# Lightning attention and a snake MLP: partition halves that hold two neighbouring blocks instead of two head groups

## The chip, the core and the metric

The kernel runs on one core of a Trainium2 chip. The metric is the device time of one execution in microseconds (us). Five engines run side by side, each through its own list of instructions in order: TensorE (PE, matmuls; PEld is its weight load), VectorE (DVE), ScalarE (ACT), GpSimd (POOL) and SyncE (SP), which here does nothing but issue transfers. The transfers themselves run on 16 DMA engines. An engine whose next instruction waits for a semaphore stands still, and everything behind that instruction in its list stands still with it.

## The reference

Four batches, eight heads, 768 positions, head width 64. Each head keeps a state of 64x64; blocks of positions are worked off in order, and the output feeds an MLP.

```
for each block of 64 positions:
    intra = ((q k^T) * lam**(i-j), lower triangle) v
    inter = (q * lam**(i+1)) state
    out   = intra + inter
    state = lam**64 * state + (k * lam**(63-j))^T v
x = out as 3072 tokens x 512 (8 heads x 64)
h = x @ w_in                       # 512 -> 2048
g = h + sin(alpha*h)**2 / (alpha + 1e-9)
result = g @ w_out                 # 2048 -> 512, float32
```

## The kernel before, in words

**Attention.** The kernel uses blocks of 128 positions: 6 to a batch (NB), 24 in all; the program calls one *s*. q is multiplied by lam**t and k by lam**-t (t is the position in the batch), so the state needs no decay and is a plain running sum. A tile of block s has 128 partitions: the lower 64 hold heads 0 to 3, the upper 64 heads 4 to 7, and each partition holds two neighbouring positions of four heads (512 B a head in float32). So load_x brings q, k and v of a block with two transfers each, one a partition half, of 64 partitions and 128 KB (lines 349 to 360). All are issued by SP; one ring of six buffers (RL) for each of q, k, v lets a load start as soon as the block six before has been read.

A block goes through these steps:

- scale_block (line 438): q and k times the table of lam powers, on POOL (on DVE for the first few), float32 to bf16; v cast to bf16, on ACT or POOL.
- piece_T (line 453): the transposes of q and k, by TensorE for blocks 0 to 11 and by a DMA transpose that SP issues for blocks 12 to 23.
- run (line 476), with up to three parts in one go of TensorE: S is q k^T of a block (then masked by DVE into Sm), O is the output of a block (Sm times v, and q times the state copy Zc), Z adds k^T v of a block to the state in PSUM bank ZB, which is then copied to Zc. In the steady part a step G(s) does S of block s, and O and Z of block s-1.

**MLP.** Tokens go in chunks of 512 (c = 0 to 5). unit_A (or unit_A2, two feature tiles of 256 tokens) is four (or eight) matmuls of x and w_in into a PSUM bank; then ACT makes the sine (t), ACT or POOL its square (u), DVE the sum (gT), which frees the bank. unit_B is four matmuls of gT and w_out; every fourth ends with a copy by ACT (osb) and a store of 256 KB.

**What sets the order.** No engine order is written out. _Plan keeps a list of operations with a duration, buffers read and written, and a lead. _order places them one by one at the time at which it reckons that each can begin: it takes loads at 0.4 us of issue on SP, and 0.47 us on the wire for a load of 128 KB. For TensorE and SP it may look 40 and 1 operations ahead; ACT, DVE and POOL take what can begin first. The lists that result are fixed: on the chip each engine follows its list, and waits where the list was too hopeful. Until the first MLP unit can run, filler matmuls (spin, line 746) are put where TensorE would idle.

**The sequence.** SP first issues the loads of blocks 0 to 3, then two of the first 512 columns of w_in (ws, line 373). The rest of w_in and all of w_out (w) are loaded by POOL once v of block 3 has landed (lines 732 to 735), and block 4 after w_in's third quarter. FIRST (line 788) mixes attention steps T4 to G12 with MLP work of chunks 0 and 1; afterwards each G has eight MLP units around it (line 809).

Of the kernel before, what the change touches and what calls it, by code (L numbers as in the profile page):

```python
# [5 lines left out]
ALU = mybir.AluOpType  # L6
# [26 lines left out]
class _Plan:  # L33
# [7 lines left out]
    EARLY = 0.0, 0.0  # L41

# [76 lines left out]
    def _order(self, lands):  # L119
# [10 lines left out]

        def ready(o):
            t = 0.0
            for d in o.deps:
                if d.done is None:
                    return None
                t = max(t, d.done + (0.0 if d.eng == o.eng else self.LAT))
            return t

        while fixed["PE"] or fixed["SP"] or free:
            best = None  # L140
            for e in ("PE", "SP"):
                can = []
                for o in fixed[e][:self.AHEAD[e]]:
                    r = ready(o)
                    if r is not None:
                        can.append((max(r, clock[e]), index[o], o, e, o.dur))
                if can:
                    soon = min(c[0] for c in can)
                    soon += self.EARLY[1] if e == "PE" and soon < self.EARLY[0] else self.SLACK
                    c = min((c for c in can if c[0] <= soon), key=lambda c: c[1])  # L150
                    if best is None or c[:2] < best[:2]:
                        best = c
            for o in free:
                r = ready(o)
                if r is None:
                    continue
                if o.port:
                    r = max(r, port)
                if isinstance(o.eng, str):
                    c = (max(r, clock[o.eng]), index[o], o, o.eng, o.dur)  # L160
                else:
                    _, e, d = min((max(r, clock[e]) + d + late, e, d) for e, d, late in o.eng)
                    c = (max(r, clock[e]), index[o], o, e, d)
                if best is None or c[:2] < best[:2]:
                    best = c
# [20 lines left out]
            if o.dma is not None:  # L186
                clock[e] = t + o.issue
                wire = max(wire, t + 0.8) + dur
                o.done = max(t + 0.8 + o.dur + o.lat, lands[o]) if o in lands else wire + o.lat
            else:  # L190
                clock[e] = o.done = t + dur
                if o.port and e != "ACT":
                    port = o.done
# [50 lines left out]
def bass_lightning_attn__then__act_snake_kernel(  # L244
# [34 lines left out]
    with es:  # L279
# [23 lines left out]
        Zc = ring("Zc", 2, [128, 4, D], BF16)  # L303
# [4 lines left out]
        lam_bc = sb("lam_bc", [128, 4], F32)  # L308
        lnlam = sb("lnlam", [128, 4], F32)
        E_i = sb("E_i", [128, 2 * NB], I32)  # L310
        E_f = sb("E_f", [128, 2 * NB], F32)
        lnL = sb("lnL", [128, NB, 4, 2], F32)
        Lq = sb("Lq", [128, NB, 4, 2], F32)
        Lk = sb("Lk", [128, NB, 4, 2], F32)
# [11 lines left out]
        def _(_unused_eng):  # L326
# [10 lines left out]
            P.EARLY = 20.0, 0.3  # L337

# [10 lines left out]
            def load_x(s, which="qkv", after=()):  # L349


                b, n, j = s // NB, s % NB, s % RL
                for x in which:
                    for r in range(2):
                        last[x, s] = load(
                            x32[x][j][half(r), :, :, :].rearrange("p h t d -> p h (t d)"),
                            {"q": q, "k": k, "v": v}[x][b, 4 * r:4 * r + 4, n * BL:(n + 1) * BL, :].rearrange(
                                "h (p t) d -> p h (t d)", t=2),
                            (x + "32", j, r), 0.47, f"{x}32{j}{r}", lat=2.7, after=after, runs=16,
                        )  # L360
# [34 lines left out]
            for r in range(2):  # L395
                load(lam_bc[half(r), :], bass.AP(lam.tensor, 4 * r, [[0, 64], [1, 4]]), ("lam", r), 0.1, f"lam{r}", "ACT", runs=1)
# [4 lines left out]
            op("POOL", lambda e: e.iota(E_i[:, :], [[128, NB], [1, 2]], base=0, channel_multiplier=2), 0.6, writes=["E_i"])  # L401
            op("POOL", lambda e: e.tensor_copy(E_f[:, :], E_i[:, :]), 0.3, ["E_i"], ["E_f"])
            op("DVE", lambda e: e.tensor_scalar_add(E_f[half(1), :], E_f[half(1), :], -128.0), 0.1, ["E_f"], ["E_f"])
# [9 lines left out]
            for r in range(2):  # L413
# [3 lines left out]
            op("ACT", lambda e: e.activation(lnlam[:, :], lam_bc[:, :], ACTF.Ln), 1.5, [("lam", 0), ("lam", 1)], ["lnlam"])  # L417
            op("DVE", lambda e: e.tensor_tensor(
                lnL[:, :, :, :], bass.AP(E_f, 0, [[2 * NB, 128], [2, NB], [0, 4], [1, 2]]),
                bass.AP(lnlam, 0, [[4, 128], [0, NB], [1, 4], [0, 2]]), ALU.mult), 0.2,  # L420
# [17 lines left out]
            def scale_block(s):  # L438


                n, jl, j = s % NB, s % RL, s % R2
                for x, i, L in ((("k", 1, Lk), ("q", 0, Lq)) if s == 0 else (("q", 0, Lq), ("k", 1, Lk))):
                    eng, dur = ("DVE", 0.7) if (s, x) in QE else ("POOL", 1.05)
                    ported(op(eng, lambda e, x=x, i=i, L=L: e.tensor_tensor(  # L444
                        qk2[:, j, i, :, :, :].rearrange("p w u d -> p u w d"),
                        bass.AP(x32[x][jl], 0, [[8 * D, 128], [4 * D, 2], [D, 4], [1, D]]),
                        bass.AP(L, n * 8, [[8 * NB, 128], [4, 2], [1, 4], [0, D]]), ALU.mult), dur,
                        [(x + "32", jl, 0), (x + "32", jl, 1), "L" + x], [(x + "2", j)]))
                op((("ACT", 0.62, 0.0), ("POOL", 1.05, 0.3)) if s > 11 else "ACT",
                   lambda e: (e.copy if e is nc.scalar else e.tensor_copy)(v2[j][:, :, :, :], x32["v"][jl][:, :, :, :]), 0.62,  # L450
                   [("v32", jl, 0), ("v32", jl, 1)], [("v2", j)])
# [24 lines left out]
            def run(S=None, O=None, Z=None, b0=3, ob=2, ob2=None, parted=False, after=()):  # L476


                if Z is not None and Z % NB == NB - 1:
                    Z = None  # L480
# [21 lines left out]
                if Z is not None:  # L502
                    for t in range(2):
                        for r, u, w in RUW:
                            (first if r else then).append(
                                (r, u, 32, (ZB, u), ps[ZB][half(u), 64 * (2 * r + w):64 * (2 * r + w) + 64],
                                 qk2[half(r), Z % R2, 1, 2 * w + t, u, :], v2[Z % R2][half(r), 2 * u + w, t, :]))
# [32 lines left out]
                if ob2 is None:  # L540
                    assert O is None or O % NB or Z == O
                begun0 = set() if Z is not None and Z % NB == 0 else {(ZB, 0), (ZB, 1)}

                def mm(e):
                    ins, begun = None, set(begun0)
                    for i, (_, _, _, key, d, w, x) in enumerate(first + early + then):
                        if first and then and i == len(first + early):
                            e.wait_ge(turn, turns[0])
                        ins = e.matmul(d, w, x, start=key not in begun, stop=True, skip_group_check=True)  # L549
# [10 lines left out]
                if O is not None:  # L560
                    reads += [("v2", O % R2), ("qT", O % RT), ("Sm", O % 2)] + ([("Zc", O % 2)] if O % NB else [])
                    writes += [bank(b) for b in obs]
                if Z is not None:
                    reads += [("k2", Z % R2), ("v2", Z % R2)]
                    if bank(ZB) not in writes:
                        writes += [bank(ZB)]
                op("PE", mm, 0.2 + max(busy.values()) / 1000, reads, writes, after=after)
# [7 lines left out]
                if Z is not None:  # L575
                    op((("ACT", 0.4, 0.0), ("DVE", 0.4, 0.0)),
                       lambda e: (e.copy if e is nc.scalar else e.tensor_copy)(  # L577
                           Zc[(Z + 1) % 2][:, :, :].rearrange("p a b -> p (a b)"), ps[ZB][:, 0:256]),
                       0.4, [bank(ZB)], [("Zc", (Z + 1) % 2), "ZB read"])
                if O is not None:  # L580
                    c, i4 = O // BPC, O % BPC
                    assert abs(obs[0] - obs[1]) == 1
                    for eng, r0, r1, dur in ((("ACT", 0, 1, 0.45), ("DVE", 1, 2, 0.4)) if parted else
# [4 lines left out]
                            bass.AP(xT[c % RX], 2 * ra * TCH + BL * i4,  # L588
                                    [[4 * TCH, 128], [2 * way * TCH, r1 - r0], [TCH, 2], [1, 2], [2, 64]]),
                            bass.AP(banks, to[ra], [[4096, 128], [way * (to[1] - to[0]), r1 - r0], [128, 2], [64, 2], [1, 64]])), dur,  # L590
                           [bank(b) for b in obs[r0:r1]], [("xT", c % RX, i4, 2 * r + u) for r in range(r0, r1) for u in range(2)] + ["ZB read"] * (r1 - 1 if ob2 is None else 0))
                    if ob2 is None:
                        op(WIPE, lambda e: e.memset(ps[ZB][:, 256:512], 0.0), 0, [("xT", c % RX, i4, 2)], [bank(ZB)])
                P_.lead = lead

            def piece_G(s, t, ob=2):
                run(S=s, O=t, Z=t, ob=ob)
# [107 lines left out]
            def prep(s):  # L705
                if s < NBLK:
                    for ahead in range(s + 2, min(s + 3, NBLK)) if s >= 10 else ():
                        load_x(ahead)
                    scale_block(s)
                    if s >= TD:  # L710
# [7 lines left out]
            run(Z=0)  # L718
            run(O=0, ob=6, ob2=7)
            run(S=1)  # L720
# [7 lines left out]
            run(S=3)  # L728
            run(O=3, ob=6, ob2=7, parted=True)
# [22 lines left out]
            for i in range(NM):  # L752
# [4 lines left out]
                if i == 3:  # L757
                    run(Z=3, after=[u])
# [16 lines left out]
            def attend(kind, s):  # L775
                ob = 2 if bi < 12 else 2 - 2 * (bi // 4 % 2)
                P.lead = 40 if s <= TD else 0
                if kind == "T":
                    piece_T(s, 0 if bi < 12 else ob)
                    P.lead = 0  # L780
                    prep(s + 2)
                else:
                    if TD <= s < NBLK:
# [24 lines left out]
            block = TD + 1  # L808
# [52 lines left out]
```

## Time and profile before

| | |
|---|---|
| median of 3 runs | 239.51 us (238.84 to 239.54) |
| the profiled execution | 240.18 us, of which the span from first to last instruction is 238.4 us |
| PE busy | 213.7 us (90%) |
| ACT, DVE, POOL busy | 150.3, 123.2, 95.9 us |
| loads of q, k, v | 144 of 128 KB, issued by SP |
| chain that ended last | PE 62%, DMA 18%, SP's queue 9%, ACT 5% |

The 40 slices of the page (5.96 us each) show three parts. In the first 24 us TensorE does little but the attention of four blocks and filler. From there to about 112 us it has gaps while the DMA engines are busy for 60% and more of the time. After that it is busy throughout, and the DMA engines have little to do.

### The profile page before, as it was taken

How to read it: one execution, taken by the hardware profiler on the slowest of the kernel's cores; microseconds unless marked ns; L12 is line 12 of the kernel's file. 1: busy time of each engine (PE TensorE's matmuls, PEld its weight loads, DVE VectorE, ACT ScalarE, POOL GpSimd, SP SyncE). 2: the span in 40 equal slices, each digit the busy share in tenths (PEclk: the TensorE clock that was granted, in tenths of full speed). 3: DMA queues.
4: the chain of work that ended last, by engine and by line, in shares of the span. 5: the costliest groups of instructions: out<-in, count | busy, mean ns of one | idle time of the engine just before them, and what ended most of it. 6: DMA issues, size and time to landing. Idle time of an engine off the chain costs nothing.

```text
span 238.4 us, 5336 instructions
## 1 busy us (share of the span) xinstructions
PE 213.7 (90%) x2214; PEld 109.6 (46%) x2214; DVE 123.2 (52%) x190; ACT 150.3 (63%) x260; POOL 95.9 (40%) x102
## 2 busy tenths in 40 slices
PE   5778899969957569996999999999999999999995
PEld 2344644434735235642454544454554444444444
DVE  2754667535654568756365465664565634443200
ACT  4533699417665668848677877667667667777312
POOL 1238468166565548646665452231323111001100
PEclk9965999999999999997999999999999999999999
DMA  4768999997676698697999889011101110111122
GB/s 114 198 167 243 207 194 215 236 236 205 174 199 175 195 265 197 177 222 173 199 185 242 207 191 149 5 47 44 45 5 44 45 47 0 44 44 48 44 88 88
DMA packets 60408, 33.39 MB, mean 140 GB/s; under 512 B 15696, under 2 KB 57440, under 8 KB 60384
## 3 DMA queue, kind: packets, MB, share of 16 engines
q1 hardware_dynamic: 53616, 24.26, 42.6%
q0 software_dynamic: 3696, 3.67, 9.5%
q10 hardware_dynamic: 3072, 5.12, 6.3%
q8 instruction: 17, 0.28, 0.5%
q14 instruction: 7, 0.06, 0.1%
HBM read 27.27 MB, written 6.29 MB: 141 GB/s over the span
## 4 chain that ended last, share of the span: by engine, by line
PE 62%; DMA 18%; SPq 9%; ACT 5%; POOL 2%; issue 2%; DVE 1%; ACTq 0%
PE bank L681 28%; PE bank L616 25%; DMA v<-in_v_dram 11%; SPq L343 8%; PE bank L549 5%; DMA q<-in_q_dram 4%; DMA k<-in_k_dram 2%; ACT v L450 2%; POOL qk L444 2%; PE bank L650 2%; PE bank L749 1%; ACT u L630 1%; SPq L456 1%; PE bank L466 1%; ACT osb L694 1%
## 5 line engine op out<-in xcount | busy, mean ns | idle before, releaser
L681 PE MATMUL bank<-w,gT 128*128 128x512 bf16 (+1 forms) x400 | 95.8, 373 | 0.0
L633 DVE SCALAR_TENSOR_TENSOR gT<-u,rinv,bank 128x512 bf16<-128x512 bf16 x80 | 58.9, 744 | 52.1 <-ACT u L630 26.8
L616 PE MATMUL bank<-xT,w 128*128 128x512 bf16 x320 | 80.9, 382 | 3.0 <-DVE gT L668 2.8
L626 ACT ACTIVATE t<-bank,alpha 128x512 bf16<-128x512 f32 x80 | 54.4, 688 | 26.4 <-PE bank L616 26.1
L631 POOL TENSOR_TENSOR u<-t 128x512 bf16<-128x512 bf16 x31 | 32.1, 1038 | 73.6 <-ACT t L626 73.5
L681 PEld LDWEIGHTS bank<-w,gT 128*128 128x128 bf16 x400 | 38.2, 98 | 40.5 <-issue 1.1
L616 PEld LDWEIGHTS bank<-xT,w 128*128 128x128 bf16 x320 | 30.9, 98 | 40.5 <-DVE gT L668 3.4
L570 DVE TENSOR_TENSOR Sm<-bank,mask 128x1024 bf16<-128x1024 f32 x24 | 29.3, 1220 | 11.6 <-PE bank L549 11.5
L444 POOL TENSOR_TENSOR qk<-q,Lq 128x512 bf16<-128x512 f32 x22 | 22.9, 1042 | 29.0 <-DMA q<-in_q_dram 28.8
L450 ACT CAST v<-v 128x512 bf16<-128x512 f32 x21 | 12.9, 615 | 33.4 <-DMA v<-in_v_dram 33.4
L630 ACT ACTIVATE u<-t 128x512 bf16<-128x512 bf16 x49 | 30.6, 629 | 1.2
L444 POOL TENSOR_TENSOR qk<-k,Lk 128x512 bf16<-128x512 f32 x23 | 24.3, 1058 | 13.5 <-DMA k<-in_k_dram 6.5
L694 ACT COPY osb<-bank 128x512 f32<-128x512 f32 (+1 forms) x25 | 14.1, 567 | 14.0 <-PE bank L681 14.0
L668 DVE SCALAR_TENSOR_TENSOR gT<-u,rinv,bank 128x256 bf16<-128x256 bf16 x32 | 13.6, 477 | 14.6 <-POOL u L665 9.0
L650 PE MATMUL bank<-xT,w 128*128 128x256 bf16 x128 | 15.7, 273 | 5.7 <-DVE gT L668 5.0
L466 PE MATMUL bank<-ident,qk 128*128 128x128 bf16 x96 | 9.3, 231 | 8.7 <-POOL qk L444 5.1
L650 PEld LDWEIGHTS bank<-xT,w 128*128 128x128 bf16 x128 | 11.8, 98 | 9.1 <-DVE gT L668 6.6
L549 PE MATMUL bank<-qkT 64*64 64x128 bf16 x384 | 15.1, 227 | 0.2 <-DVE qkT L471 0.2
L660 ACT ACTIVATE t<-bank,alpha 128x256 bf16<-128x256 f32 x32 | 13.3, 471 | 2.5 <-PE bank L650 2.4
L549 PE MATMUL bank<-v,qk 64*64 64x64 bf16 x320 | 12.0, 196 | 0.7 <-ACT Zc L577 0.3
L466 PEld LDWEIGHTS bank<-ident,qk 128*128 128x128 bf16 x96 | 5.9, 102 | 13.3 <-POOL qk L444 7.1
L587 DVE CAST xT<-bank 128x512 bf16<-128x512 f32 (+1 forms) x10 | 7.0, 702 | 9.3 <-PE bank L549 8.6
(49 smaller groups left out, 129.6 us busy)
## 6 DMA issues: line engine op xcount, KB each, us to landing
q<-in_q_dram SPq DMA_DIRECT2D x48, 128.0 KB, 3.1
k<-in_k_dram SPq DMA_DIRECT2D x48, 128.0 KB, 3.2
v<-in_v_dram SPq DMA_DIRECT2D x48, 128.0 KB, 3.2
out_dram<-osb ACTq DMA_DIRECT2D x19, 256.0 KB, 2.0
w<-in_moe_w_out_dram POOLq DMA_DIRECT2D x4, 512.0 KB, 13.4
w<-in_moe_w_in_dram POOLq DMA_DIRECT2D x3, 512.0 KB, 7.1
ws<-in_moe_w_in_dram SPq DMA_DIRECT2D x2, 512.0 KB, 5.0
out_dram<-osb SPq DMA_DIRECT2D x4, 256.0 KB, 4.4
```

The lines of the kernel that those rows point to most:

```text
L343: return op(eng, lambda e: e.dma_start(dst, src), dur, dma=sem, lat=lat, after=after, issue=issue, runs=runs, writes=key if isinstance(key ...
L444: ported(op(eng, lambda e, x=x, i=i, L=L: e.tensor_tensor(qk2[:, j, i, :, :, :].rearrange("p w u d -> p u w d"), bass.AP(x32[x][jl], 0, [[ ...
L450: lambda e: (e.copy if e is nc.scalar else e.tensor_copy)(v2[j][:, :, :, :], x32["v"][jl][:, :, :, :]), 0.62,
L549: ins = e.matmul(d, w, x, start=key not in begun, stop=True, skip_group_check=True)
L570: op("DVE", lambda e: e.tensor_tensor(Sm[S % 2][:, :, :, :].rearrange("p u w i -> p (u w i)").rearrange("p (a b) -> p a b", b=256), banks[ ...
L616: ins = e.matmul(ps[hb][:, c0:c1], w1[:, kc, 128 * m:128 * (m + 1)], xT[x][:, kc, c0:c1], start=(kc == 0 and c0 == lo), stop=(kc == NKC - ...
L626: op("ACT", lambda e: e.activation(t16[ju][:, w], ps[hb][:, w], ACTF.Sin, scale=alpha[:, m:m + 1]), 0.69 * f, [bank(hb), "alpha"], [("t16" ...
L630: lambda e: (e.activation(u16[ju][:, w], t16[ju][:, w], ACTF.Square) if e is nc.scalar else e.tensor_tensor(u16[ju][:, w], t16[ju][:, w], ...
L631: e.tensor_tensor(u16[ju][:, w], t16[ju][:, w], t16[ju][:, w], ALU.mult)), 0,
L633: op("DVE", lambda e: e.scalar_tensor_tensor(out=gT[g][:, m, w], in0=u16[ju][:, w], scalar=rinv[:, m:m + 1], in1=ps[hb][:, w], op0=ALU.mul ...
L650: ins = e.matmul(ps[hb][:, 256 * i:256 * i + 256], w1[:, kc, 128 * (m + i):128 * (m + i + 1)], xT[x][:, kc, lo:lo + 256], start=(kc == 0 a ...
L681: ins = e.matmul(ps[ob][:, w], gT[g][:, m, 128 * s4:128 * (s4 + 1)], w2[:, m, w], start=(m == 0), stop=(m == NM - 1),)
```

## The change

A tile's lower 64 partitions now hold the first, the upper 64 the second of two neighbouring blocks of 128 positions, for one group of four heads. The index s runs over (pair of blocks n, head group g): s // 2 counts pairs and s % 2 is the group. There are still 24 steps, and q, k and v of a step are still 256 KB each, but one load brings them.

What follows from it in the code: the table of lam powers has other strides and the same size; in O the second block (r = 1) uses the state after the first, and the first (r = 0) that of the step two before, so Zc has three buffers and Z is in two parts: G(s) adds the first block of step s (before: of s-1), and the second block of step s-1. A state copy is made in all 24 steps (before: in 20). The output tile xT of a step now covers two blocks of four heads. The planner reckons 0.93 us of wire for a load, models the port that DVE and POOL share with a new function begins, and has a table LATER whose values are all 0.

```
-                for x in which:
-                    for r in range(2):
-                        last[x, s] = load(
-                            x32[x][j][half(r), :, :, :].rearrange("p h t d -> p h (t d)"),
-                            {"q": q, "k": k, "v": v}[x][b, 4 * r:4 * r + 4, n * BL:(n + 1) * BL, :].rearrange(
-                                "h (p t) d -> p h (t d)", t=2),
-                            (x + "32", j, r), 0.47, f"{x}32{j}{r}", lat=2.7, after=after, runs=16,
+                for x in which:
+                    last[x, s] = load(
+                        x32[x][j][:, :, :, :].rearrange("p h t d -> p h (t d)"),
+                        {"q": q, "k": k, "v": v}[x][b, 4 * g:4 * g + 4, 256 * n:256 * n + 256, :].rearrange(
+                            "h (p t) d -> p h (t d)", t=2),
+                        (x + "32", j), 0.93, f"{x}32{j}", lat=2.7, after=after, runs=32,
...
-        Zc = ring("Zc", 2, [128, 4, D], BF16)
+        Zc = ring("Zc", 3, [128, 4, D], BF16)
...
-                if Z is not None and Z % NB == NB - 1:
-                    Z = None
+                Zo = Z - 1 if Z is not None and Z and (Z - 1) % NB < NB - 2 else None
...
-                if O is not None and O % NB:
+                if O is not None:
                     for r, u, w in RUW:
-                        (first if r == u else then).append(
-                            (u, w, 56, (obs[r], w), out_of(r, u, w).rearrange("p (t x) -> p t x", t=2),
-                             Zc[O % 2][half(u), 2 * r + w, :], q_of(O, r, u, w)))
+                        if r or O % NB > 1:
+                            (first if r == u else then).append(
+                                (u, w, 56, (obs[r], w), out_of(r, u, w).rearrange("p (t x) -> p t x", t=2),
+                                 Zc[(O + r - 1) % 3][half(u), 2 * (O % 2) + w, :], q_of(O, r, u, w)))
...
             def piece_G(s, t, ob=2):
-                run(S=s, O=t, Z=t, ob=ob)
+                run(S=s, O=t, Z=s, ob=ob)
...
+        def begins(o, e, r):
+            t = max(r, clock[e])
+            if e == "DVE" and o.port:
+                t = max(t, clock["POOL"])
+            if e == "POOL":
+                t = max(t, port)
+            return t
```

SP's list, the end of the loads of the first four blocks and what follows (the number is the buffer; x2 is two transfers in a row). Before:

```order
L343 DMA q_3<-in_q_dram 64x4x128 x2
L343 DMA k_3<-in_k_dram 64x4x128 x2
L343 DMA v_3<-in_v_dram 64x4x128 x2
L343 DMA ws<-in_moe_w_in_dram 128x4x256 x2
L343 DMA q_4<-in_q_dram 64x4x128 x2
```

Now:

```order
L357 DMA q_3<-in_q_dram 128x4x128
L357 DMA k_3<-in_k_dram 128x4x128
L357 DMA v_3<-in_v_dram 128x4x128
L357 DMA ws<-in_moe_w_in_dram 128x4x256 x2
L357 DMA q_4<-in_q_dram 128x4x128
```

SP's list keeps its order to the end; each pair of loads is one instruction.

ACT's list in the stretch in which chunk 1's first units (t and u) stand between the v casts of blocks 9 to 11 (buffers v_3 to v_5). Before:

```order
L450 CAST v_3<-v_3 128x512
L660 ACTIVATE t_0<-bank,alpha 128x256 x2
L660 ACTIVATE t_1<-bank,alpha 128x256
L664 ACTIVATE u_0<-t_0 128x512
L660 ACTIVATE t_1<-bank,alpha 128x256
L450 CAST v_4<-v_4 128x512
L577 CAST Zc<-bank 128x256
L587 CAST xT<-bank 128x4x2x64
L660 ACTIVATE t_3<-bank,alpha 128x256 x2
L450 CAST v_5<-v_5 128x512
```

Now:

```order
L461 CAST v_3<-v_3 128x512
L672 ACTIVATE t_1<-bank,alpha 128x256 x2
L672 ACTIVATE t_2<-bank,alpha 128x256
L676 ACTIVATE u_1<-t_1 128x512
L672 ACTIVATE t_2<-bank,alpha 128x256
L461 CAST v_4<-v_4 128x512
L672 ACTIVATE t_3<-bank,alpha 128x256 x2
L676 ACTIVATE u_3<-t_3 128x512
L461 CAST v_5<-v_5 128x512
```

The v casts stand where they stood, one between each few pieces of MLP work; the names of the MLP buffers have shifted by one unit.

TensorE's list in one attention step: G(8), which does O of block or step 7 (Sm, v_1) and S of 8 (qkT). Before:

```order
L549 MATMUL bank<-Sm,v_1 64x128 x16
L549 MATMUL bank<-qkT,Zc 64x128 x4
L549 MATMUL bank<-v_1,qk 64x64 x8
L549 MATMUL bank<-qkT 64x128 x12
L549 MATMUL bank<-qkT,Zc 64x128 x4
L549 MATMUL bank<-v_1,qk 64x64 x2
```

Now:

```order
L560 MATMUL bank<-Sm,v_1 64x128 x16
L560 MATMUL bank<-qkT,Zc 64x128 x2
L560 MATMUL bank<-v_1,qk 64x64 x8
L560 MATMUL bank<-qkT 64x128 x12
L560 MATMUL bank<-qkT,Zc 64x128 x2
L560 MATMUL bank<-v_2,qk 64x64 x2
```

The second part of the state now comes from v_2, the v of the same step 8, where it came from that of block 7. Over the whole program TensorE's list has the same matmuls by kind and count (384, 384, 160 and 320 in the attention, 96 transposes, 848 in the MLP), but 15 filler matmuls instead of 21.

## Rows read from the trace of the kernel before

**Rows 1.** Busy time by stretch; columns as in its first line.
```profile
core 0: us, PE busy (x) PEld busy (x) DVE busy (x) ACT busy (x) POOL busy (x), PEclk, DMA share, GB/s
3.50:13.00 9.50, 7.88 (x78) 3.47 (x76) 5.56 (x10) 6.13 (x11) 1.74 (x2) 1.00 0.72 199
...
30.00:47.00 17.00, 16.94 (x113) 8.08 (x112) 11.39 (x18) 13.01 (x24) 9.72 (x10) 1.00 1.20 214
47.00:50.00 3.00, 0.65 (x18) 0.37 (x8) 1.23 (x1) 0.30 (x1) 1.50 (x2) 1.00 1.22 241
...
64.40:85.60 21.20, 13.34 (x250) 8.80 (x243) 11.08 (x22) 11.66 (x26) 12.67 (x14) 1.00 0.70 189
85.60:103.50 17.90, 16.23 (x221) 8.91 (x220) 14.46 (x23) 15.57 (x29) 10.90 (x12) 1.00 0.78 214
...
112.00:238.40 126.40, 123.78 (x1044) 59.53 (x1042) 57.90 (x81) 83.07 (x134) 34.76 (x34) 1.00 0.36 87
```

**Rows 2.** Waits of all engines from 44 to 112 us: total, times, longest.
```profile
ACT v L450 <- DMA v<-in_v_dram: 24.8, 12, 3.3
POOL qk L444 <- DMA q<-in_q_dram: 18.4, 14, 5.5
DVE gT L668 <- POOL u L665: 9.0, 6, 4.0
```

**Rows 3.** TensorE in order of time: start, length, what; in brackets the wait ahead.
```profile
75.08 1.05 PE L650 MATMUL bank<-xT,w 128*128 128x256 bf16 x8 [1.55 <-DVE gT L668]
...
99.33 0.42 PE L549 MATMUL bank<-Sm,v 64*64 64x128 bf16 x16
...
109.92 1.89 PE L616 MATMUL bank<-xT,w 128*128 128x512 bf16 x4 [1.86 <-DVE gT L668]
```

**Rows 4.** ACT's casts of v of blocks 9, 14 and 17, with the wait ahead.
```profile
64.43 0.62 ACT L450 CAST v<-v 128x512 bf16<-128x512 f32 x1 [2.21 <-DMA v<-in_v_dram]
...
85.63 0.62 ACT L450 CAST v<-v 128x512 bf16<-128x512 f32 x1 [2.13 <-DMA v<-in_v_dram]
...
106.48 0.62 ACT L450 CAST v<-v 128x512 bf16<-128x512 f32 x1 [3.25 <-DMA v<-in_v_dram]
```

**Rows 5.** SP's queue in order of time: start, length, what is issued.
```profile
0.81 1.49 SPq L343 DMA_DIRECT2D q<-in_q_dram  x2
...
17.98 1.16 SPq L343 DMA_DIRECT2D ws<-in_moe_w_in_dram  x2
...
36.81 4.14 SPq L343 DMA_DIRECT2D k<-in_k_dram  x2
...
81.66 1.27 SPq L343 DMA_DIRECT2D v<-in_v_dram  x2
...
91.64 1.34 SPq L456 DMA_TRANSPOSE qkT<-qk  x1
```

**Rows 6.** Tile q: time from issue to landing.
```profile
DMA to landing us min/median/max: 2.6/3.1/14.4
```

**Rows 7.** Chain that ended last, in order of time: start, length, what.
```profile
13.56 4.25 DMA q<-in_q_dram
...
17.88 1.05 POOL qk L444
...
24.98 1.85 PE bank L650 x16
...
109.92 1.89 PE bank L616 x4
...
113.43 0.86 PE bank L616 x4
```

**Rows 8.** First blocks on POOL and ACT: start, length, what; in brackets the wait.
```profile
12.67 1.04 POOL L444 TENSOR_TENSOR qk<-q,Lq 128x512 bf16<-128x512 f32 x1 [4.61 <-DMA q<-in_q_dram]
...
20.74 0.62 ACT L450 CAST v<-v 128x512 bf16<-128x512 f32 x1 [3.75 <-DMA v<-in_v_dram]
```

**Rows 9.** Transfers by kind: the transposes, count, median us from issue to landing.
```profile
qkT<-qk SPq DMA_TRANSPOSE x12, 4.2
```

More of the change, by code (lines that the diff above doesn't have):

```diff
@@ L41 @@
     EARLY = 0.0, 0.0
+    LATER = {}
     LAT = 0.2
@@ L152, in _order @@
                         best = c
+            can = {}
             for o in free:
@@ L156, in _order @@
                     continue
-                if o.port:
-                    r = max(r, port)
                 if isinstance(o.eng, str):
-                    c = (max(r, clock[o.eng]), index[o], o, o.eng, o.dur)
+                    c = (begins(o, o.eng, r), index[o], o, o.eng, o.dur)
                 else:
-                    _, e, d = min((max(r, clock[e]) + d + late, e, d) for e, d, late in o.eng)
-                    c = (max(r, clock[e]), index[o], o, e, d)
+                    _, e, d = min((begins(o, e, r) + d + late, e, d) for e, d, late in o.eng)
+                    c = (begins(o, e, r), index[o], o, e, d)
+                can.setdefault(c[3], []).append(c)
+            for e, cs in can.items():
+                soon = min(c[0] for c in cs) + self.LATER.get(e, 0.0)
+                c = min((c for c in cs if c[0] <= soon), key=lambda c: c[1])
                 if best is None or c[:2] < best[:2]:
@@ L191, in _order @@
                 clock[e] = o.done = t + dur
-                if o.port and e != "ACT":
+                if o.port and e == "DVE":
                     port = o.done
@@ L337, in _ @@
             P.EARLY = 20.0, 0.3
+            P.LATER = {"ACT": 0.0, "DVE": 0.0, "POOL": 0.0}
             def bank(i):
@@ L394, in _ @@
             last = {}
-            for r in range(2):
-                load(lam_bc[half(r), :], bass.AP(lam.tensor, 4 * r, [[0, 64], [1, 4]]), ("lam", r), 0.1, f"lam{r}", "ACT", runs=1)
+            load(lam_bc[:, :], bass.AP(lam.tensor, 0, [[0, 128], [1, H]]), "lam", 0.1, "lam", "ACT", runs=1)
             load(alphaT[:, :], bass.AP(moe_alpha.tensor, 0, [[128, NM], [1, 128]]), "alphaT", 0.1, "alphaT", "ACT", lat=4.9, runs=1)
@@ L560, in run @@
                 if O is not None:
-                    reads += [("v2", O % R2), ("qT", O % RT), ("Sm", O % 2)] + ([("Zc", O % 2)] if O % NB else [])
+                    reads += [("v2", O % R2), ("qT", O % RT), ("Sm", O % 2)] + [("Zc", O % 3)] + ([("Zc", (O - 1) % 3)] if O % NB > 1 else [])
                     writes += [bank(b) for b in obs]
                 if Z is not None:
-                    reads += [("k2", Z % R2), ("v2", Z % R2)]
+                    reads += [(x, z % R2) for x in ("k2", "v2") for z in (Z, Zo) if z is not None]
                     if bank(ZB) not in writes:
                         writes += [bank(ZB)]
-                op("PE", mm, 0.2 + max(busy.values()) / 1000, reads, writes, after=after)
+                op("PE", mm, (0.25 if first and then else 0.2) + max(busy.values()) / 1000, reads, writes, after=after)
                 lead, P_.lead = P_.lead, -20
@@ L728, in _ @@
             run(S=3)
+            run(Z=3)
             run(O=3, ob=6, ob2=7, parted=True)
```

88 lines of the change are left out of this document (45 added, 43 removed).

## The prediction

> **What bounds the kernel now.** I read the busy times by stretch first [rows 1]. From 112 us on TensorE is busy for 123.78 of 126.40 us and the DMA share is 0.36: nothing that a load does is seen there, and the change keeps TensorE's list of matmuls there by kind and count. What can move lies ahead of 112 us, in three places. From 3.5 to 13 us the DMA engines carry 199 GB/s at a share of 0.72. From 30 to 50 us their share is 1.20 and more: they are full with weights and loads, and TensorE stands still for 2.35 of the 3 us from 47 to 50. From 64.4 to 85.6 us TensorE works 13.34 of 21.20 us, and yet the DMA share is only 0.70. That last stretch is the odd one: a gap, and no engine or DMA that is full.
>
> The waits say why [rows 2]. In 44 to 112 us ACT waits 24.8 us for v, in 12 waits, and POOL 18.4 us for q. Neither cast is urgent, but both engines take their lists in order: the sines and squares that stand behind the cast are late, then DVE waits for u, and TensorE for the bank that gT frees, as at 75.08 us (1.55 us) and at 109.92 us (1.86 us) [rows 3]. The casts of v of blocks 9 to 14 begin at 64.43 and 85.63 us: six casts, five gaps, 4.24 us each [rows 4].
>
> What spaces them is SP's queue [rows 5]. A pair of loads takes 1.27 us there and the next begins 0.04 us later, so one load costs (1.27 + 0.04) / 2 = 0.66 us, and a block's six 3.9 us. The wire is faster: 199 GB/s at a share of 0.72 and 189 at 0.70 make 270 to 276 GB/s at a full share, so 128 KB take 0.475 us and a block's 768 KB 2.85 us. SP's queue is the bound of the loads wherever the DMA share is about 0.7; in 30 to 50 us it is the wire, as a pair of loads that takes 4.14 us to issue at 36.81 us shows.
>
> **The change part by part.** *The loads.* 144 issues become 72. What does an issue of 256 KB in 512 pieces cost? The row for it is the load of ws: 512 KB each, in 512 pieces of 1 KB, two in 1.16 us, so 0.58 us [rows 5]. The price thus goes by the instruction and not by its pieces. The upper bound is twice that of now, 1.3 us, if it went by pieces. I take 0.66 us, as it is the nearest row with that number of pieces. Then a block takes 2.0 us of SP and 2.85 us of wire, and the wire sets the pace: 1.1 us per block less in the stretches at 0.7.
>
> The Trainium skill, "DMA: Bandwidth & Descriptors", section "Issuing engines are not separate DMA queues", says that the time a sequencer needs to initiate a DMA is usually small relative to the DMA itself. By that rule halving the issues would be worth nothing, and the sum would be about zero. The trace does not agree here: 0.66 us of issue against 0.475 us of wire.
>
> *Front, to the first MLP unit.* A load's smallest time to landing is 2.6 us [rows 6], of which 0.475 is wire, so 2.1 us are fixed. From the first issue at 0.81 us and 0.95 us of wire per 256 KB, the n-th load lands at 2.9 + 0.95 n. q of block 2 (n = 7) lands at 9.6 instead of about 12.67 us [rows 8], 3.1 us sooner; q of block 3 (n = 10) at 12.4 instead of 13.56 + 4.25 = 17.8 us [rows 7], 5.4 sooner; v of block 3 (n = 12) at 14.3 instead of about 20.7 us [rows 8], 6.4 sooner. v of block 3 also releases POOL's loads of weights, and the two of ws stand right behind it on SP, so the weights come sooner by as much. The chain runs from q of block 3 over POOL to the first MLP unit at 24.98 us [rows 7]. What is late next is DVE, which has masks, copies and scalings of four blocks to do one after the other and no longer waits between them. I take 5.0 us, with 3.1 and 6.4 as bounds.
>
> *30 to 50 us.* The wire is full; the same bytes go over it, only sooner. Nothing more is gained, and the gap at 47 us stays.
>
> *64.4 to 85.6 us.* Five gaps of 4.24 us become five of 2.85 us: 5 x 1.39 = 7.0 us. TensorE needs 13.34 us there, the wire 14.25 us: the next bound is close behind, so the gain can't be much over 7.9 us (TensorE's whole idle time), and is 0 if an issue should cost 1.3 us. I take 7.0.
>
> *85.6 to 112 us.* TensorE idles for 1.67 us in the first part [rows 1] and for 1.86 us at 109.92 us, behind the cast of v of block 17, for which ACT waited 3.25 us [rows 4]. After that stop eight matmuls take 113.43 - 109.92 = 3.51 us where two groups of 0.86 take 1.72 [rows 7]: TensorE runs at the lower of its two clocks, 1.2 GHz, and loses another 1.8 us. SP has a transpose of 1.34 us per block there too, so a block costs it 5.3 us, and 3.3 us after the change. All of it is 5.3 us, none is 0; I take half, 2.5 us, since the transposes share the wire and the MLP work around comes sooner as well.
>
> *Edits that I cost at nothing.* Four more state copies, each of half the elements of a v cast of 0.62 us [rows 4], lie beside TensorE's work; without that cover they cost 2.5 us at most. The scalings and casts keep number and size. Z of step s reads v of s, one step sooner: behind a waiting G(s) all of TensorE's list is queued. From 64 us the casts of v run blocks ahead of their G: v of block 14 is cast at 86 us, and G(13) begins at 99.33 us [rows 3]. Only G(4) to G(7), in the full stretch of the wire, may wait: at most one load of 0.95 us and a cast of 0.62 us each. There the gap at 47 us may grow a little; I leave it in the range. The planner's port model and its table of zeros change the order of few instructions, and TensorE has 6 filler matmuls fewer, which lay in waits anyway.
>
> The sum goes against the profiled execution: 240.18 us, span 238.4 us. 5.0 + 7.0 + 2.5 = 14.5 us, so 225.7 us. The median of the runs is 239.51 us, 0.7 us under that execution, so I predict 225.0 us. The bounds of the terms are 3.1 + 0 + 0 (236.4 us against the median) and 6.4 + 7.9 + 5.3 = 19.6 us (219.9 us); the gap at 47 us on top would make 217.5 us.
>
> **The rivals.** *Only the front gains.* The loads of 64 to 112 us are sooner, but the lists of ACT and POOL were made by the planner, and a cast waits for landing wherever the list puts it; if MLP work there waits for one another and not for loads, TensorE's gaps stay. For it: POOL and ACT are busy for 12.67 and 11.66 of 21.2 us, far from idle. Against it: the wait that ended last is a v or a q in most cases, 43 us of them. Price: 5.0 us, 234.5 us.
>
> *All gaps go.* The planner's 0.93 us on the wire is now what the wire gives (0.95 us), while before its 0.4 us of issue was 0.66 in truth; lists made with true times would leave hardly a wait. For it: that agreement. Against it: the full wire in 30 to 50 us, which the planner sees too. 19.6 us, 220 us.
>
> *No effect.* This is the page's rule (issue hidden anyway), or an issue whose cost goes by pieces: 256 KB would cost 1.3 us of SP, and every landing stays. Against it: the ws row. 239.5 us.
>
> *Slower: transposes behind a deeper queue.* With SP no longer the brake, loads pile up ahead of the transposes of steps 12 to 23, which share its queue. A transpose lands 4.2 us after issue [rows 9]; behind one more block it lands 2.85 us later, at 7.05. That of block 13 is issued at 91.64 us [rows 5] and G(13) begins at 99.33 us: 7.7 us of room. Up to that it is free; beyond it every G waits. Once two blocks are ahead (9.9 us), 2.2 us are lost in each of 12 steps, 26 us, less the 14.5 gained: 251 us; the point from which it makes the kernel slower is 1.2 us of wait per step. Against it: the ring of six buffers lets a load begin only when a block has been read, so a pile can't last.
>
> **How the numbers follow.** My forecast has 0.60 (222 to 229 us), only the front 0.16 (232 to 236), all gaps 0.13 (217.5 to 221.5), no effect 0.05, slower 0.06. The range 219 to 235 us holds the first, most of the second and of the third, and leaves out just under 2 in 10. Faster by over 0.3%, which is about what a measurement of this kernel can tell from no change, are the first three: 0.89. No effect is 0.05, slower 0.06.
>
> **What would show it.** In the profile after: single issues of about 0.66 us by SP, or longer ones with a DMA share near 1 where it was 0.7; v of block 3 cast by about 15 us; the first MLP unit by about 20 us; gaps of about 3 us between the casts of v of steps 9 to 14, and ACT's waits for v well under 24.8 us; TensorE without a gap from about 97 us on, instead of 112. The forecast is wrong if an issue takes 1.2 us or more without the wire being full, if TensorE's gaps of 1.5 us before MLP units are still there with u or gT as the cause and no load behind them, or if G steps wait for qkT or for v.

## The result and the profile after

| | before | after |
|---|---|---|
| median of the runs | 239.52 us (238.84 to 240.88) | 221.54 us (220.83 to 222.08) |
| the profiled execution | 240.18 us, span 238.4 | 221.84 us, span 220.1 |
| PE, share of the span | 90% | 94% |
| chain that ended last | PE 62%, DMA 18%, SP's queue 9% | PE 84%, DMA 6%, SP's queue 2% |

The ratio is 0.924, with an interval of 0.919 to 0.929: the kernel is 18.0 us faster. The forecast was 14.5 us. An execution more than 1.5% above the fastest of its kernel (one, of extra_issue) is left out here and below. Five points of the program, found in both traces, say where the time came from:

| point in the program | before, us | after, us | gained since the point above | forecast |
|---|---|---|---|---|
| first MLP unit begins | 24.98 | 19.68 | 5.3 | 5.0 |
| the run of MLP units without a gap begins | 30.66 | 26.23 | -0.9 | 0 |
| first unit of chunk 1 | 60.22 | 52.52 | 3.3 | 0 |
| first unit of chunk 2 | 96.63 | 82.18 | 6.75 | 7.0 |
| last instruction ends | 238.4 | 220.1 | 3.85 | 2.5 |

The points do not all lie behind the same work. Before, one attention step more stands between the second and the third point: TensorE is busy there for 26.38 us before and for 25.53 us after, so 0.85 of the 3.3 us is work that now comes later. The idle time of TensorE in the rows below and in [rows 1] is the safer measure, and the account at the end goes by it.

The busy times by stretch, with the columns of [rows 1]; the stretches are cut at about the same work as there, not at the same times:

```profile
3.50:13.00 9.50, 7.57 (x107) 3.78 (x105) 5.75 (x11) 5.45 (x11) 3.45 (x3) 1.00 1.12 286
26.00:43.00 17.00, 17.00 (x117) 8.16 (x115) 10.92 (x18) 12.43 (x23) 12.45 (x13) 1.00 1.18 236
43.00:46.00 3.00, 3.00 (x20) 1.46 (x20) 1.92 (x2) 0.99 (x2) 2.52 (x4) 1.00 1.09 293
46.00:60.00 14.00, 13.24 (x263) 9.07 (x262) 9.43 (x17) 11.74 (x23) 12.00 (x12) 1.00 1.12 294
60.00:75.00 15.00, 13.19 (x257) 8.67 (x250) 11.75 (x21) 12.47 (x27) 10.03 (x11) 1.00 1.08 269
75.00:94.00 19.00, 19.00 (x247) 10.89 (x242) 13.17 (x23) 16.35 (x32) 14.93 (x15) 1.00 1.17 265
98.00:220.10 122.10, 119.47 (x1018) 57.59 (x1016) 55.85 (x77) 82.55 (x134) 27.52 (x28) 1.00 0.27 72
```

The DMA share, 0.70 to 0.72 where SP's queue was the bound [rows 1], is now over 1 in every stretch shown up to 94 us, and the same DMA engines ("the wire" from here on) move 265 to 294 GB/s where loads dominate. The three microseconds in which TensorE had stood still for 2.35 us are full (43 to 46 us), and the last stretch has kept its 2.6 us of idle time.

SP's queue, in order of time:

```profile
0.81 0.44 SPq L357 DMA_DIRECT2D q<-in_q_dram  x1
...
2.39 0.51 SPq L357 DMA_DIRECT2D q<-in_q_dram  x1
...
3.99 1.39 SPq L357 DMA_DIRECT2D v<-in_v_dram  x1
5.42 0.74 SPq L357 DMA_DIRECT2D q<-in_q_dram  x1
...
75.04 0.51 SPq L357 DMA_DIRECT2D k<-in_k_dram  x1
```

A load of 256 KB is issued in 0.44 to 0.51 us where nothing presses on the queue (the first four, and again at 75 us), against 1.27 us for a pair [rows 5]. From the fifth to the twelfth load an issue takes 0.74 us and more; these eight go out in 7.8 us, 0.97 us each, which is about the time of 256 KB on a full wire, so the queue seems to wait for the wire there. The waits of 40 to 112 us; the window begins earlier than that of [rows 2], because the same work now comes earlier, and for the kernel before both windows give the same sums:

```profile
POOL qk L455 <- DMA q<-in_q_dram: 7.4, 8, 3.1
ACT v L461 <- DMA v<-in_v_dram: 6.9, 5, 3.0
```

ACT's wait for v has gone from 24.8 to 6.9 us, POOL's for q from 18.4 to 7.4. The casts of v of steps 9 to 12; [rows 4] has 9, 14 and 17:

```profile
54.83 0.62 ACT L461 CAST v<-v 128x512 bf16<-128x512 f32 x1
...
57.66 0.61 ACT L461 CAST v<-v 128x512 bf16<-128x512 f32 x1
...
61.20 0.62 ACT L461 CAST v<-v 128x512 bf16<-128x512 f32 x1 [1.11 <-DMA v<-in_v_dram]
...
63.64 0.62 ACT L461 CAST v<-v 128x512 bf16<-128x512 f32 x1 [0.47 <-DMA v<-in_v_dram]
```

The distance is (63.64 - 54.83) / 3 = 2.94 us where it was 4.24, and only two of the four still wait for their load. TensorE, in order of time:

```profile
17.85 0.28 PE L560 MATMUL bank<-qkT 64*64 64x128 bf16 x7
19.29 0.39 PE L560 MATMUL bank<-qkT 64*64 64x128 bf16 x9 [1.16 <-issue]
19.61 3.50 PE L662 MATMUL bank<-xT,w 128*128 128x256 bf16 x16
...
24.48 1.91 PE L662 MATMUL bank<-xT,w 128*128 128x256 bf16 x16 [0.64 <-DVE xT L598]
...
43.80 0.39 PE L477 MATMUL bank<-ident,qk 128*128 128x128 bf16 x4
...
73.12 1.04 PE L628 MATMUL bank<-xT,w 128*128 128x512 bf16 x4 [0.72 <-DVE gT L680]
```

The wait of 0.72 us at 73.12 us, for gT, is the last ahead of an MLP unit; the stops at 75 and 110 us [rows 3] have gone. A new one stands at the top: 1.16 us for which the profile names no releaser, and behind it a granted clock of 0.50 (from 20 to 22 us), the lower of TensorE's two levels, 1.2 GHz. The first 16 matmuls of the MLP take 3.50 us there; the next 16 take 1.91 us.

### The profile page after: what moved, and what is told of

Read it like the earlier page. It is cut to its first block, busy times and chain, and to the rows that moved or that the text cites. A ratio compares the mean times of both kernels' runs of the same rounds, so it can differ in the third digit from the quotient of the medians.

```text
span 220.1 us, 5194 instructions
## 1 busy us (share of the span) xinstructions
PE 207.9 (94%) x2208; PEld 108.9 (49%) x2208; DVE 121.2 (55%) x186; ACT 153.5 (70%) x267; POOL 94.3 (43%) x102
## 4 chain that ended last, share of the span: by engine, by line
PE 84%; DMA 6%; DVE 3%; SPq 2%; ACT 2%; POOL 1%; issue 1%
PE bank L693 36%; PE bank L628 31%; PE bank L560 9%; PE bank L662 5%; DMA v<-in_v_dram 3%; DMA q<-in_q_dram 2%; SPq L357 2%; DVE Sm L581 2%; PE bank L477 2%; POOL qk L455 1%; DVE xT L598 1%; DVE gT L680 1%; ACT t L672 1%; ACT xT L598 1%; POOL u L677 0%
## 5 line engine op out<-in xcount | busy, mean ns | idle before, releaser
L628 PE MATMUL bank<-xT,w 128*128 128x512 bf16 x320 | 79.7, 379 | 0.7 <-DVE gT L680 0.7
L643 POOL TENSOR_TENSOR u<-t 128x512 bf16<-128x512 bf16 x28 | 29.0, 1039 | 77.1 <-ACT t L638 76.7
L628 PEld LDWEIGHTS bank<-xT,w 128*128 128x128 bf16 x320 | 31.0, 98 | 38.1 <-DVE gT L680 1.4
L642 ACT ACTIVATE u<-t 128x512 bf16<-128x512 bf16 x52 | 32.6, 629 | 1.3
L662 PE MATMUL bank<-xT,w 128*128 128x256 bf16 x128 | 17.4, 290 | 1.4 <-DVE xT L598 1.4
L461 ACT CAST v<-v 128x512 bf16<-128x512 f32 x20 | 12.3, 616 | 9.0 <-DMA v<-in_v_dram 9.0
L662 PEld LDWEIGHTS bank<-xT,w 128*128 128x128 bf16 x128 | 12.7, 104 | 4.6 <-DVE xT L598 1.3
L677 POOL TENSOR_TENSOR u<-t 128x512 bf16<-128x512 bf16 x10 | 10.3, 1039 | 7.2 <-ACT t L672 7.2
L598 ACT CAST xT<-bank 128x512 bf16<-128x512 f32 (+1 forms) x17 | 12.2, 718 | 0.2 <-PE bank L560 0.2
L560 PE MATMUL bank<-qkT,Zc 64*64 64x128 bf16 x160 | 11.3, 228 | 0.3
```

Source lines behind the costliest of these rows:

```text
L598: op(eng, lambda e, r0=r0, r1=r1, ra=ra, way=way: (e.copy if e is nc.scalar else e.tensor_copy)(bass.AP(xT[c % RX], a * TCH + BL * (i4 + r ...
L628: ins = e.matmul(ps[hb][:, c0:c1], w1[:, kc, 128 * m:128 * (m + 1)], xT[x][:, kc, c0:c1], start=(kc == 0 and c0 == lo), stop=(kc == NKC - ...
L642: lambda e: (e.activation(u16[ju][:, w], t16[ju][:, w], ACTF.Square) if e is nc.scalar else e.tensor_tensor(u16[ju][:, w], t16[ju][:, w], ...
L643: e.tensor_tensor(u16[ju][:, w], t16[ju][:, w], t16[ju][:, w], ALU.mult)), 0,
L662: ins = e.matmul(ps[hb][:, 256 * i:256 * i + 256], w1[:, kc, 128 * (m + i):128 * (m + i + 1)], xT[x][:, kc, lo:lo + 256], start=(kc == 0 a ...
```

## The experiments

All are timed against the kernel before, which ran beside them, and the ratios are to it. "Over after" is the median less the 221.54 us of the changed kernel. The runs were taken in four sets, in which the median of the kernel before lay between 238.3 and 239.9 us, so differences of under 1 us in "over after" say nothing.

**The loads in two halves again: all, the first four steps, the others.** The planner still reckons 0.93 us, and the lists of the engines stay word for word those of the changed kernel.

```
+    parts = [slice(0, 64), slice(64, 128)]   # split_front: if s < 4; split_rest: if s >= 4
-    dma_start(x32[x][j], from_[b, heads of g, 256 positions])
+    for w in parts:
+        dma_start(x32[x][j][w], from_[b, heads of g, 128 positions of w])
```

> The changed kernel with each load of 256 KB issued as two transfers of 64 partitions and 128 KB, one right behind the other, on the same semaphore; the lists of all engines stay as in the changed kernel. Theory A (the gain is the issue time that SP saves): SP needs 1.3 us per load again, the DMA share falls to about 0.7 between weights and transposes, first MLP unit at about 25 us, time 234 to 240 us. Theory B (the gain comes from the regrouping: new lists, the state one step sooner): stays at 220 to 224 us. Theory C (a transfer of 64 partitions uses the wire worse, whatever its issue costs): as A in time, but with a DMA share near 1.

Measured: 240.83 us, 1.0085 (1.0043 to 1.0128). The times by stretch, with the columns of [rows 1]:

```profile
3.50:13.00 9.50, 6.80 (x69) 3.10 (x67) 5.24 (x10) 5.03 (x10) 1.35 (x2) 1.00 0.71 201
...
60.00:75.00 15.00, 11.06 (x165) 7.43 (x167) 8.07 (x15) 8.66 (x19) 9.44 (x10) 0.89 0.67 188
```

SP's queue, and the waits of all engines from 40 to 112 us:

```profile
2.25 1.27 SPq L358 DMA_DIRECT2D k<-in_k_dram  x2
```

```profile
ACT v L466 <- DMA v<-in_v_dram: 24.9, 12, 5.0
```

The loads are as before: 1.27 us for a pair, a share of 0.67 to 0.71, 24.9 us of waits for v; the time is 0.8 us above the 234 to 240 us expected. So the whole gain hangs on the form of the loads. Theory B, by which a part would have stayed, is out, and so is theory C, by which the share would have been near 1. The new grouping with the new lists and loads in halves is even 1.0 to 3.1 us slower than the kernel before.

> The same split for the loads of steps 0 to 3 only. Theory A: first MLP unit at about 25 us instead of 19.7, a full wire from 30 us on as before, time 4.4 to 5.5 us over the changed kernel, 226 to 227 us. Theory B: 220 to 223 us.

Measured: 226.76 us, 0.9482 (0.9433 to 0.9530), 5.2 us over after. TensorE and POOL, in order of time:

```profile
27.33 1.91 PE L667 MATMUL bank<-xT,w 128*128 128x256 bf16 x16 [0.65 <-DVE xT L603]
```

```profile
47.00 1.04 POOL L460 TENSOR_TENSOR qk<-q,Lq 128x512 bf16<-128x512 f32 x1 [4.84 <-DMA q<-in_q_dram]
```

The second 16 matmuls of the MLP are 2.85 us later than in the changed kernel (24.48), but the scaling of q of step 5 is 4.8 us later (42.23 there, below). The front's gain is therefore paid out twice: at the first units and again behind them, where TensorE is busy for only 2.22 of the 3 us from 43 to 46 us here.

> The same split for the loads of steps 4 to 23 only. Theory A: first MLP unit at 19.7 us as in the changed kernel, then waits of ACT for v of 20 us and more, TensorE's gaps back between 45 and 105 us, 9 to 14 us over the changed kernel, 231 to 236 us; and where weights and loads fill the wire (26 to 42 us) it makes no difference, if the form of a transfer does not matter there. Theory B: 220 to 224 us.

Measured: 236.12 us, 0.9847 (0.9775 to 0.9919), 14.6 us over after, just above the 9 to 14 us expected. TensorE:

```profile
43.79 0.39 PE L482 MATMUL bank<-ident,qk 128*128 128x128 bf16 x4
```

These are the transposes of step 5, at the place of the old gap at 47 us. They begin at 43.79 us without a wait, as in the changed kernel (43.80), though all later loads are slow here. Up to the first unit of chunk 1, from the run of units without a gap on, TensorE idles 3.18 us in the kernel before, 2.63 in split_all, 2.31 in split_front, 1.39 here and 0.76 in the changed kernel. So the new lists alone fill little of that stretch, and the quick loads of the first four steps fill most of it. The two parts add up: 5.2 + 14.6 = 19.8 us, against 19.3 us for all; by the ratios, 5.8 + 14.5 against 20.2 us.

**A second issue that brings next to nothing; and two issues of 128 partitions.** extra_issue keeps each load and adds a transfer of 512 B (16 partitions of 32 B) into a tile that nobody reads, and the load counts as landed when both have landed. split_heads cuts each load by heads, so that both halves reach all 128 partitions.

```
+    extra[:, e8:e8 + 8] <- from_[b, 4 * g, 256 * n:256 * n + 16, 0:8]         # extra_issue
+    for i in (0, 1): x32[x][j][:, 2 * i:2 * i + 2] <- heads 2 * i, 2 * i + 1  # split_heads
```

> The changed kernel with its loads of 128 partitions, but each followed on SP by a transfer of 512 B (16 partitions of 32 B into a tile that nobody reads): twice the issues, the same bytes and the same form of load. Theory A (issue time of SP): as split_all, 234 to 240 us. Theory C (form of the transfer) and theory B: 220 to 225 us.

Measured: 228.25 us, 0.9539 (0.9473 to 0.9605). SP's queue:

```profile
1.86 0.42 SPq L359 DMA_DIRECT2D k<-in_k_dram  x1
2.32 0.50 SPq L359 DMA_DIRECT2D extra<-in_k_dram  x1
```

The time lies between the two ranges expected, 220 to 225 and 234 to 240 us. The upper one took 0.62 us for each issue, whatever it carries, which makes 1.24 us a load. The rows say 0.42 us for the load and 0.50 for the small one, with the steps between them 1.01 us a load, only a little over what the wire needs for 256 KB. Since a load has landed here only with its small transfer, the run does not part the slower pace from the later landing; both come from the second issue.

> The changed kernel with each load issued as two transfers of 128 partitions, two heads and 128 KB each: as many issues and bytes as in split_all, the same lists, but all partitions in each transfer. Theory A1 (an issue costs SP about 0.62 us whatever its form): 1.3 us of SP per load, DMA share about 0.7, 237 to 242 us as split_all. Theory A2 (an issue over 128 partitions costs 0.42 us and one over 64 costs 0.62): 2 x 0.46 = 0.92 us per load, about what the wire needs (0.90 us), 221 to 227 us.

Measured: 230.20 us, 0.9614 (0.9554 to 0.9673). SP's queue:

```profile
1.81 0.97 SPq L358 DMA_DIRECT2D k<-in_k_dram  x2
```

The time lies between the two ranges expected here too, 221 to 227 and 237 to 242 us: theory A1 is out, and theory A2 had the price nearly right (0.92 us a load, 1.02 measured) and the time 3 us too low. Two issues of 128 KB that reach 128 partitions take 0.97 us, two of 64 partitions 1.27 us. The price goes by the form. Ordered by SP's time for one load, the steps between issues included, the runs make a series:

| kernel | SP per load, us | what carries | us |
|---|---|---|---|
| after | 0.49 to 0.55 | the wire sets the pace, 0.90 | 221.5 |
| extra_issue | 1.01 | 256 KB and 512 B | 228.3 |
| split_heads | 1.02 | 2 x 128 KB | 230.2 |
| split_all | 1.31 | 2 x 128 KB | 240.8 |

The two in the middle move different bytes in their second issue and cost SP the same, and their times are close to each other. The time goes by what a load costs SP, once this exceeds the wire's time.

**The kernel before, with its planner told the true issue.** Loads and grouping stay as they were; only the lists change.

```
-    (x + "32", j, r), 0.47, ..., lat=2.7, after=after, runs=16,
+    (x + "32", j, r), 0.47, ..., lat=2.7, after=after, runs=16, issue=0.66,
```

> The kernel before, where only the planner reckons 0.66 us of SP per load of q, k, v instead of 0.4: same transfers, other lists of ACT, DVE, POOL and TensorE. Theory A (the pace of the loads is the cost, whatever the list): 236 to 241 us. Theory D (the cost was that the lists put casts too early, and a list made with the true pace saves most of the 18 us): 223 to 232 us.

Measured: 234.74 us, 0.9822 (0.9751 to 0.9893). The waits from 40 to 112 us:

```profile
ACT v L450 <- DMA v<-in_v_dram: 15.9, 10, 3.4
```

ACT's waits for v fall by 9 us without any load being issued more quickly, and the time by 4.3 us (2.6 to 6.0). So a part of what slow loads cost went with the lists, and the waits point to casts that stood too early in them. It is one list against another; four lists for the changed kernel, below, lie within 1.8 us. The time lies between what the two theories said (236 to 241, and 223 to 232): neither was right alone.

**The weights earlier.** The two loads of ws, ahead of the loads of step 3, or ahead of its v alone.

```
-    load_x(3); load_w1_first()
+    load_w1_first(); load_x(3)                        # ws_before_3
+    load_x(3, "qk"); load_w1_first(); load_x(3, "v")  # ws_before_v3
```

> The changed kernel with the two loads of ws issued ahead of the loads of step 3 instead of behind them (lists made anew). If the first MLP unit waits for ws, it starts at 17 to 18 us instead of 19.7 and the time falls by 1 to 2 us, 219 to 221 us; if the front is bound by the attention of step 3, whose loads land 3.6 us later, the time is 222 to 225 us.

> As ws_before_3, but only v of step 3 comes behind the loads of ws. By the same two readings 219 to 221 us, or 221.5 to 224 us.

Measured: 225.58 us, 0.9421 (0.9370 to 0.9471), and 225.75 us, 0.9414 (0.9356 to 0.9472), both about 4 us slower than the changed kernel and 0.6 and 1.8 us above the slower of the two ranges expected. In ws_before_3 the first MLP unit begins at 16.11 us, 3.6 us sooner, but the second batch at 23.66 us and the run of units at 26.35 us, no sooner than in the changed kernel (26.23). From 43 to 60 us TensorE has gaps of 2.5 us, with waits for v (0.87 us) and xT (1.63 us). A sooner first unit bought nothing; steps 3 to 5 came later, and that seems to be what was paid for.

**The planner's figures for a load.** The changed kernel once more, and with 1.00 or 0.90 us of wire, or 3.2 us to landing.

```
-    (x + "32", j), 0.93, ..., lat=2.7
+    (x + "32", j), 1.00 (plan_wire_100) or 0.90 (plan_wire_090), ... or lat=3.2 (plan_lat_32)
```

> The changed kernel once more, beside the three below on the same chip: 220 to 223 us, ratio to the kernel before 0.92 to 0.93.

> The changed kernel, where only the planner reckons 1.0 us of wire per load instead of 0.93 (other lists, same transfers). If the casts that still wait for loads (ACT 6.9 us, POOL 7.4 us from 40 to 98 us) cost TensorE its last gaps there (2.6 us), a later place in the lists saves 1 to 2.5 us: 219 to 220.5 us. If those gaps come from elsewhere: within 1.5 us of the changed kernel, on either side.

> As plan_wire_100 with 0.90 us, which is what the wire gave to loads alone. If lists that are too hopeful cost time, it is slower by up to 2 us, 221.5 to 224 us; otherwise within 1.5 us of the changed kernel.

> As plan_wire_100, with 0.93 us of wire kept and 3.2 instead of 2.7 us from the end of the wire to landing for a load in the planner's reckoning. By the same reading 219 to 221 us, or within 1.5 us of the changed kernel.

Measured: 221.87 us, 0.9296 (0.9255 to 0.9338); 221.17 us, 0.9271 (0.9229 to 0.9314); 222.95 us, 0.9345 (0.9299 to 0.9390); 221.91 us, 0.9300 (0.9240 to 0.9360). The intervals overlap, but the scatter of the kernel before is in each of them. Beside one another on one chip, all runs with 0.90 us (222.52 to 223.54) are slower than all of the changed kernel (221.51 to 222.09) and all with 1.00 us (220.92 to 221.69), by 1.1 and 1.8 us in the mean. So the more hopeful list cost half a per cent here, though 0.90 us is what the wire gave to loads alone. The other three overlap one another, and no version is known to beat the changed kernel.

## Why the prediction was right, and where it was not

**The number.** 221.54 us lies inside the stated range of 219 to 235 us, but 3.5 us under the 225.0 us predicted and just under the span of the main forecast (222 to 229 us); the rival *all gaps go*, 220 us, came closer. By TensorE's idle time and clock the terms came out as 4.4 us in front (5.3 less 0.9; 5.0 forecast), 2.4 us in 30 to 50 us (0), 6.0 us in 64.4 to 85.6 us (7.0) and 5.3 us in 85.6 to 112 us (2.5). Two terms were too small and two too large; that the sum missed by only 3.5 us is in part luck.

**The mechanism held.** SP's queue set the pace of the loads and the wire sets it now. split_all gives all of the gain back with the lists unchanged; extra_issue and split_heads show that the time follows SP's price of a load. That also answers the rule of the Trainium skill, "DMA: Bandwidth & Descriptors", section "Issuing engines are not separate DMA queues", by which an issue is usually small beside its DMA: for these loads it was the larger of the two (0.66 against 0.475 us), and split_all, which puts it back, costs 19.3 us.

**The price of an issue.** The text took 0.66 us for 256 KB and had 1.3 us as upper bound. It is 0.44 to 0.51 us. The text took 0.66 us as the nearest row with 512 pieces, but that is the price of a load of 64 partitions in 256 pieces; the row with 512 pieces and 128 partitions is the load of ws, 0.58 us [rows 5]. The sum did not change by it, as the wire is slower than either.

**The wire.** 0.95 us for 256 KB was forecast and 0.90 us (286 to 294 GB/s) came. Rates worked out from a share of 0.7 were 5% low.

**Front.** 5.0 us forecast, 5.3 at the first unit; quick loads of the first four steps are worth 5.2 us in the end by split_front, with what they do behind 30 us in it. v of block 3 is cast at 15.25 us (about 15 forecast, 20.74 before), the first unit begins at 19.68 us (about 20 forecast). The low clock that begins there, which no step of the forecast had, took 1.6 us (16 matmuls in 3.50 instead of 1.91 us); as 0.7 us of attention work now stands ahead of the first unit, 0.9 us of the 5.3 were gone when the units ran without a gap.

**The step that failed: 30 to 50 us.** "Nothing more is gained, and the gap at 47 us stays." The gap went, 2.4 us. The rows that answer to it are the scaling of q of step 5 on POOL, and TensorE's transposes behind it, before:

```profile
48.42 1.04 POOL L444 TENSOR_TENSOR qk<-q,Lq 128x512 bf16<-128x512 f32 x1 [5.51 <-DMA q<-in_q_dram]
```

```profile
49.52 0.40 PE L466 MATMUL bank<-ident,qk 128*128 128x128 bf16 x4 [2.35 <-POOL qk L444]
```

and the scaling now; the transposes are the row at 43.80 us above:

```profile
42.23 1.04 POOL L455 TENSOR_TENSOR qk<-q,Lq 128x512 bf16<-128x512 f32 x1 [3.10 <-DMA q<-in_q_dram]
```

It came 6.2 us sooner, while TensorE's MLP work ahead of it came only 4.4 us sooner. The difference of 1.8 us, and four MLP matmuls (0.9 us, at 42.92 us) that the new list puts ahead of these transposes, close a gap of 2.35 us. The text was right that the wire is full there and that the same bytes go over it. But it shifted both sides by the same amount, the loads and TensorE, and they shift apart: the wire's queue moves by what the loads gained, TensorE by what the chain to the first unit gained. split_rest shows that the quick front does it with all later loads slow.

**64.4 to 85.6 us.** 7.0 us forecast. TensorE's idle time fell from 7.86 us to 1.81 (60 to 75 us), 6.0 us; the 6.75 us between the points has gaps behind 85.6 us in it. Casts of v came every 2.94 us (2.85 forecast). The working held, and the term was 1 us too large.

**85.6 to 112 us.** Half of 5.3 us was taken, 2.5. All of it came, which makes this the largest miss: from 75.00 to 98.00 us TensorE has no gap, and there is no stop and no low clock like those behind 110 us any more. The 3.85 us of the table leave out the gaps ahead of 96.63 us. "Without a gap from about 97 us" was too cautious: from 74 us. The fear that the transposes and the loads would crowd one another did not come true.

**The edits at nothing.** No cost of theirs is seen in the changed kernel: the Z of step 4 has its v cast at 41.10 us and G(4) begins at 42.3. That this is cover and not a free edit is seen where the loads are slow. TensorE's waits in split_front:

```profile
PE bank L565 <- ACT v L466: 1.2, 1, 1.2
```

In split_all it is 0.8 us there. "At most one load and a cast" for G(4) to G(7) was the right size, and it may be what makes split_all slower than the kernel before; that was not tried by itself.

**The rivals.** *All gaps go* (220 us) came closest, but 2.6 us of gaps are left from 46 to 75 us. *Only the front* is out by split_rest, which lacks 14.6 us. *No effect* is out by the result. *Slower by the transposes:* they land later, as expected, 4.2 us [rows 9] becoming 5.1; transfers by kind in the changed kernel:

```profile
qkT<-qk SPq DMA_TRANSPOSE x12, 5.1
```

but the 7.7 us of room were enough: no G waits for one. What the forecast lacked as a term of its own, and had only as a reason of *all gaps go*, is the planner: before, it reckoned 0.4 us for an issue of 0.66, and before_true_issue puts 4.3 us on that. The change made the planner's figure nearly true by the way (0.93 us against 0.90 measured).

## What to carry to other kernels

Where an engine issues transfers back to back and the DMA share stays at 0.7, compare the issue's time with the wire's for the same bytes; merging issues paid here until the wire was the slower of the two; that it pays nothing beyond that was not tried. When loads come sooner, move each consumer by its own amount: a gap lies between two chains, and it closes if they shift differently, even where no more bytes per second can be had. And look at what a planner believes of a load: lists that were too hopeful seem to have cost time by themselves.

## What the runs showed of the hardware that was not expected

The time that SP needs for an issue goes by form more than by bytes: 0.62 us for 64 partitions (128 KB), 0.42 to 0.51 for 128 partitions (256 KB), 0.47 for 128 partitions (128 KB), 0.50 for 16 partitions of 32 B. By what in the form it goes is open.

TensorE stopped for 1.16 us at about 18 us in the midst of a run of equal matmuls, with no releaser in the profile. The traces point to its own instructions. The page of the changed kernel has a DMA queue for instructions, and TensorE runs 4416 of the 5194 that it counts:

```profile
q8 instruction: 17, 0.28, 0.5%
```

The first of these 17 packets, 16 KB each, is on the move from 16.68 to 17.78 us, among the loads. In six runs TensorE stops at the same place of its list, behind the first 449 matmuls and weight loads, and goes on 1.3 to 1.5 us after the first packet has landed: for 1.16 us in the changed kernel, 0.74 in after_again, 1.09 in split_rest, 1.01 in plan_wire_090, and 0.35 and 0.42 in plan_wire_100 and plan_lat_32. In split_all, split_front, extra_issue and split_heads the packet had landed 5 to 7.5 us before TensorE came to that place, and there is no stop. No run was aimed at it, so this is a reading and not shown by an experiment.

The low clock does not simply follow from that stop. In the changed kernel the granted clock is 0.50 behind it, which made 16 matmuls take 3.50 instead of 1.91 us, and they took 3.27 us in after_again; in plan_wire_090, with a stop of 1.01 us, the clock from 20 to 22 us is 1.00 and they take 1.99 us. What decided it is open.
